# One planned order for loads, weights and the f32 loads of pairs 8 to 11, one release per pair, and x of batch 1 transposed on TensorE

## Chip, cores and metric

One core of one Trainium2 chip. The metric is the device time of an execution in microseconds. "Time" is the median of an execution's runs; "span" is the length of the profiled execution from its first to its last instruction, which in these runs is 1.8 us less than that same execution's time (321.0 and 322.81 for the kernel before). The profiled run of the kernel before is one of its slower ones, so spans and medians differ a little. Each ratio compares a kernel with the kernel before on the same chip in the same rounds. The experiments ran on four chips (runs 1 to 8, 9 to 15, 16 and 17, 18), and the changed kernel was timed only in the first comparison, so an experiment is set beside it by ratios, across rounds. Every experiment was correct unless it is said to be wrong on purpose.

## The reference

Attention with random positive features (32 pairs of heads), whose output is the input x of a two-layer network with a sigmoid gate:

```python
def phi(x):                                   # q and k scaled by D**-0.25
    proj = np.einsum('bhsd,md->bhsm', x, omega)   # 128 features of 64 columns
    h = proj - np.sum(x * x, axis=-1, keepdims=True) / 2.0
    return np.exp(h - np.max(h, axis=-1, keepdims=True)) / np.sqrt(m)
kv  = np.einsum('bhsm,bhsd->bhmd', k_p, v);  z = np.sum(k_p, axis=2)
num = np.einsum('bhsm,bhmd->bhsd', q_p, kv)
den = np.einsum('bhsm,bhm->bhs', q_p, z)[..., None] + 1e-06
# x = num / den, heads side by side: 4608 tokens x 512
h = x @ w_in                                  # 512 x 2048
return (h / (1.0 + np.exp(-1.702 * h))) @ w_out   # 2048 x 512
```

q, k and v are (8, 8, 576, 64), all f32.

## The kernel before

The kernel is made by a small planner in Python that runs when the kernel is built. It knows every operation, what it depends on, on which engines it can go and how long it takes there, and simulates the whole kernel. What it hands on is only the order of operations on each engine; on the chip each engine runs its own list strictly in order, and waits where data are missing.

One operation of the planner, by its name, for a pair i of heads: `hk`, `hq`, `hv` (f32 loads of k, q, v, pairs 8 on, issued by SyncE), `cast` (to bf16, ScalarE or VectorE), `TD` (q and k transposed by a DMA, issued by SyncE), `K`, `Q`, `KV`, `ND` (TensorE), `xm` (x of the pair into `xb`), `XD` (x transposed by a DMA into `xt`), `m1` and `m2` (four matmuls of the first and the second layer), `st` (a store, SyncE). `ld` are the loads that GpSimd issues: pairs 1 to 7 and the eight weight quarters `wi` and `wo`.

```python
QUEUE = {"hk": 4.5, "hq": 4.5, "hv": 4.5, "TD": 4.5, "XD": 3.0}  # issue to landing
ENGINES = {                                    # us on each engine that may do it
    "m1": {"P": 0.864}, "m2": {"P": 0.864},  # ... cut
    "TD": {"S": 1.6}, "XD": {"S": 1.2}, "st": {"S": 0.9},
    "hk": {"S": 0.9}, "hq": {"S": 0.9}, "hv": {"S": 0.9},
    "cast": {"D": 0.740, "A": 1.010},        # ... cut
}
LOADS = [("k", 1), ("q", 1), ("k", 2), ("q", 2), ("k", 3), ("q", 3), ("v", 0), ("v", 1), ("v", 2), ("v", 3)]
LOADS += [("wi", j) for j in range(4)]
LOADS += [(x, i) for i in range(4, 8) for x in "kqv"] + [("wo", j) for j in range(4)]
XDMA, TDMA = 6, 8          # from this pair on x, and q and k, are transposed by DMA
JOIN, AHEAD = 16, 2        # from this pair on Q, KV and K(+2) are one burst
# ... in schedule():
    deps["gate", 8] = [("ld", "wo", 0)]       # all f32 loads wait for w_out's first quarter
    for i in range(EARLY, NPAIR):
        deps["hk", i] = [("hv", i - 1) if i > EARLY else ("gate", 8)] + ([("cast", i - NSTG)] if i - NSTG >= EARLY else [])
        deps["cast", i] = [("hk", i), ("hq", i)] + [("TD" if i - NSTQ >= TDMA else "TQ", i - NSTQ)]
# ... issued from emit(), shortened:
def TD(i):                                     # runs on SyncE's queue
    nc.sync.dma_start_transpose(t[:], qk_t[i][:])
def XD(i):
    nc.sync.dma_start_transpose(dst, xb)
```

The softmax here doesn't subtract the row's maximum and nothing guards it: scores larger than these inputs give would overflow.

## Time and profile before

| | before |
|---|---|
| time, median of the runs | 320.94 us (319.98 to 322.03) |
| span of the profiled run | 321.0 us |
| TensorE busy, mean granted clock | 97%, 0.998 |
| DMA | 51.69 MB, 161 GB/s over the span |

The prediction below shows the page's slices, windows and waits and how to read them. One view it does not show is that of the DMA issues (what, queue, count, KB, median us from issue to landing):

```profile
win<-in_moe_w_in_dram POOLq DMA_DIRECT2D x4, 512.0 KB, 11.3
wout<-in_moe_w_out_dram POOLq DMA_DIRECT2D x4, 512.0 KB, 10.0
```

### The profile page before, as it was taken

Reading aid. Unit: us, or ns where it says so; the run is one execution under the profiler, and the core shown is the slowest. Engines: PE = TensorE matmul, PEld = TensorE weight load, DVE = VectorE, ACT = ScalarE, POOL = GpSimd, SP = SyncE. Lnnn points to the kernel's source line nnn. Section 1 sums busy time; section 2 is a strip of 40 time slices with the busy share of each in tenths; the row PEclk is TensorE's granted clock in tenths of the full one; section 3 lists DMA queues with packets and bytes.
Section 4 is the critical chain, followed back from the end, with each engine's and each line's share of the span. In section 5 each row is a group of like instructions: output and inputs, shape, how many; then the busy total and the mean of one; then the engine's idle time right before and its main releaser. Section 6 shows DMA issues by size and latency. Waiting matters only on the chain.

```text
span 321.0 us, 6636 instructions
## 1 busy us (share of the span) xinstructions
PE 310.8 (97%) x2567; PEld 152.2 (47%) x2567; DVE 179.6 (56%) x341; ACT 202.2 (63%) x379; POOL 59.9 (19%) x98
## 2 busy tenths in 40 slices
PE   6899999999999999999999999999999999999995
PEld 3565554444454444444444454444444444444444
DVE  2878854688558946574666556554635344344300
ACT  3957975788789667866688567666654434434411
POOL 8946311311131211111102030212010000000000
PEclk9999999999999999999999999999999999999999
DMA  8999989999999999999999472323022121111133
GB/s 171 271 222 263 207 253 306 146 300 259 285 191 239 261 242 251 243 237 266 289 263 257 71 134 39 74 54 88 20 56 53 35 59 39 35 33 34 33 88 78
DMA packets 69663, 51.69 MB, mean 161 GB/s; under 512 B 49024, under 2 KB 55168, under 8 KB 69632
## 3 DMA queue, kind: packets, MB, share of 16 engines
q1 hardware_dynamic: 62384, 42.25, 56.4%
q0 software_dynamic: 6880, 8.62, 13.8%
q8 instruction: 20, 0.33, 0.5%
q10 hardware_dynamic: 368, 0.39, 0.4%
q14 instruction: 11, 0.09, 0.1%
HBM read 36.73 MB, written 9.44 MB: 144 GB/s over the span
## 4 chain that ended last, share of the span: by engine, by line
PE 74%; DMA 16%; DVE 3%; issue 2%; ACT 2%; POOL 1%; SPq 1%; ACTq 0%; DVEq 0%; POOLq 0%
PE mo L695 17%; PE mo L721 16%; PE trB L721 12%; PE tr L695 8%; PE trB L695 6%; DMA stg<-in_q_dram 5%; PE tr L721 5%; DMA v<-in_v_dram 4%; DMA wout<-in_moe_w_out_dram 2%; PE nd L657 2%; PE nd L639 2%; DMA stg<-wout 2%; PE pqk L561 2%; DMA xt<-xb 1%; DMA om_f<-in_omega_dram 1%
## 5 line engine op out<-in xcount | busy, mean ns | idle before, releaser
L721 PEld LDWEIGHTS <-gT 128*128 128x128 bf16 x592 | 55.8, 98 | 61.9 <-issue 0.5
L695 PEld LDWEIGHTS <-win 128*128 128x128 bf16 x576 | 53.2, 98 | 61.3 <-issue 2.7
L695 PE MATMUL mo<-xt,win 128*128 128x512 bf16 x316 | 80.2, 379 | 0.4 <-DMA xt<-xb 0.3
L721 PE MATMUL mo<-wout,gT 128*128 128x512 bf16 (+1 forms) x304 | 71.4, 368 | 0.0
L705 ACT ACTIVATE th<-mo 128x512 bf16<-128x512 f32 x79 | 47.5, 606 | 33.9 <-PE mo L695 33.7
L709 DVE SCALAR_TENSOR_TENSOR gT<-th,mo 128x512 bf16<-128x512 bf16 x79 | 53.1, 677 | 27.6 <-ACT th L705 27.3
L721 PE MATMUL trB<-wout,gT 128*128 128x512 bf16 x208 | 51.6, 379 | 0.0
L627 POOL CAST vp<-em 128x9 bf16<-128x9 f32 x31 | 7.3, 235 | 167.8 <-DVE em L619 139.2
L628 POOL TENSOR_TENSOR vp<-v,em 128x576 bf16<-128x576 f32 x31 | 36.0, 1161 | 0.2 <-issue 0.2
L695 PE MATMUL tr<-xt,win 128*128 128x512 bf16 x132 | 33.9, 379 | 0.0
L709 DVE SCALAR_TENSOR_TENSOR gT<-th,tr 128x512 bf16<-128x512 bf16 x33 | 22.5, 681 | 20.3 <-ACT th L705 20.3
L579 ACT ACTIVATE ke<-pqk 128x1024 bf16<-128x1024 f32 x31 | 32.7, 1055 | 0.9 <-PE pqk L561 0.9
L695 PE MATMUL trB<-xt,win 128*128 128x512 bf16 x128 | 32.9, 379 | 0.3 <-DVE gT L709 0.3
L610 DVE TENSOR_TENSOR hm<-ke 128x576 bf16<-128x576 bf16 x32 | 15.8, 492 | 30.5 <-ACT ke L579 29.1
L705 ACT ACTIVATE th<-tr 128x512 bf16<-128x512 f32 x33 | 19.8, 599 | 20.3 <-PE tr L695 20.3
L709 DVE SCALAR_TENSOR_TENSOR gT<-th,trB 128x512 bf16<-128x512 bf16 x32 | 21.8, 680 | 9.9 <-ACT th L705 9.8
L705 ACT ACTIVATE th<-trB 128x512 bf16<-128x512 f32 x32 | 19.4, 608 | 11.4 <-PE trB L695 11.4
L674 DVE TENSOR_TENSOR xb<-nd,r 128x640 bf16<-128x640 f32 x30 | 24.3, 811 | 0.8 <-ACT qe L571 0.5
L614 DVE TENSOR_REDUCE m<-hm 128x9 f32<-128x576 bf16 x32 | 23.9, 747 | 0.3
L541 ACT ACTIVATE qk<-stg 128x1152 bf16<-128x1152 f32 x13 | 15.2, 1168 | 8.3 <-DMA stg<-in_q_dram 8.3
L721 PE MATMUL tr<-wout,gT 128*128 128x512 bf16 x80 | 19.6, 379 | 0.0
L543 DVE CAST qk<-stg 128x1152 bf16<-128x1152 f32 x11 | 8.3, 754 | 18.1 <-DMA stg<-in_q_dram 18.1
(83 smaller groups left out, 283.1 us busy)
## 6 DMA issues: line engine op xcount, KB each, us to landing
out_dram<-osb SPq DMA_DIRECT2D x70, 128.0 KB, 2.4
stg<-in_k_dram SPq DMA_DIRECT2D x25, 288.0 KB, 4.0
stg<-in_q_dram SPq DMA_DIRECT2D x24, 288.0 KB, 4.5
v<-in_v_dram SPq DMA_DIRECT2D x24, 288.0 KB, 4.0
v<-in_v_dram POOLq DMA_DIRECT2D x8, 288.0 KB, 5.6
win<-in_moe_w_in_dram POOLq DMA_DIRECT2D x4, 512.0 KB, 11.3
wout<-in_moe_w_out_dram POOLq DMA_DIRECT2D x4, 512.0 KB, 10.0
qk<-in_k_dram POOLq DMA_DIRECT2D x7, 144.0 KB, 5.6
```

What stands on the lines that cost most here:

```text
L541: nc.scalar.activation(out=dst, in_=src, func=AF.Copy)
L543: nc.vector.tensor_copy(out=dst, in_=src)
L579: nc.scalar.activation(out=st[i]["ke"][:, 1:9, :].rearrange("p (j e) f -> p e j f", e=2), in_=pk[:].rearrange("p e (j f) -> p e j f", f=12 ...
L610: nc.vector.tensor_tensor(out=hm[:], in0=ke[:, :, 0:64], in1=ke[:, :, 64:128], op=ALU.max)
L614: nc.vector.reduce_max(out=m[:], in_=st[i]["hm"][:], axis=AX.X)
L627: e.tensor_copy(out=t[:, :, 64], in_=em[:])
L628: e.tensor_tensor(out=t[:, :, 0:64], in0=v_t[i][:], in1=em[:].unsqueeze(2).to_broadcast([128, NS, 64]), op=ALU.mult,)
L674: nc.vector.tensor_tensor(out=xb[:].rearrange("p g e d -> p e g d"), in0=v4[:, :, :, 0:64], in1=r[:].unsqueeze(3).to_broadcast([128, 2, NG ...
L695: nc.tensor.matmul(dst, lhsT=win[:, c, f * 128 : (f + 1) * 128], rhs=xt[c][:, n * 512 : (n + 1) * 512], start=(c == 0), stop=(c == NC_ - 1),)
L705: nc.scalar.activation(out=t[:], in_=src, func=AF.Tanh, scale=0.851)
L709: nc.vector.scalar_tensor_tensor(out=gts[n][:, f, :], in0=t[:], scalar=1.0, in1=src, op0=ALU.add, op1=ALU.mult)
L721: nc.tensor.matmul(dst, lhsT=gts[n][:, f, m * 128 : (m + 1) * 128], rhs=wout[:, f, w], start=(f == 0), stop=(f == NFC - 1),)
```

## The change

The intent: start the f32 loads of pairs 8 to 11 earlier, between the weights, each pair released by its own load of the planned order; give SyncE's work the durations of a bare issue and model the DMA queue by its service rate (`RING`), so that SyncE's list can be packed tighter; do more attention before the first layer; join Q, KV and K into one burst from pair 8 on; transpose x of pairs 6 and 7 on TensorE. The core of the diff (start-up details, single turns and placements cut):

```diff
-QUEUE = {"hk": 4.5, "hq": 4.5, "hv": 4.5, "TD": 4.5, "XD": 3.0}
+RING = {"hk": 0.85, "hq": 0.85, "hv": 0.85, "TD": 1.1, "XD": 0.65, "st": 0.75}
-    "TD": {"S": 1.6},  "XD": {"S": 1.2},  "st": {"S": 0.9},
-    "hk": {"S": 0.9},  "hq": {"S": 0.9},  "hv": {"S": 0.9},
+    "TD": {"S": 1.4},  "XD": {"S": 1.3},  "st": {"S": 1.2},
+    "hk": {"S": 0.47}, "hq": {"S": 0.47}, "hv": {"S": 0.47},
-LOADS = [("k", 1), ("q", 1), ...                       # as above
+LOADS = "k1 q1 k2 q2 k3 v0 v1 v2 q3 k4 v3 v4 k5 q4 k6 v5 q5 wi0 k7 q6 v6 q7 v7 wi1 wo0 wi2 wi3 wo1 wo2 wo3"
-BEGIN, SPACING = 8, 8
-XDMA, TDMA = 6, 8
+BEGIN = [1, 4, 12, 12, 13, 14, 17, 25, 48, 59, 60, 73, ...]   # one per pair from 8 on
+GATES = {8: 17, 9: 17, 10: 26, 11: 29}                 # pair: number of the load that releases it
+XDMA, TDMA = 8, 8
-JOIN, AHEAD = 16, 2
+JOIN, AHEAD = 8, 2
@@ schedule()
-    deps["gate", 8] = [("ld", "wo", 0)]
+    for i, n in GATES.items():
+        deps["gate", i] = [("ld", *LOADS[n])]
...
+        if kind in RING:
+            busy = st["dma"] > start                   # are GpSimd's loads still coming?
+            if busy and kind not in ("TD", "XD"):
+                st["dma"] += RING[kind]                # loads delay them; transposes do not
+            st["hw"] = max(st["hw"], start + 1.3) + RING[kind] * ((6.0 if kind in ("TD", "XD") else 1.7) if busy else 1.0)
@@ gate()
-            nc.sync.dma_start(stg[EARLY][:].bitcast(BF16)[:, 2 * S : 2 * S + 2], wout[:, 0, 0:2])
+            nc.gpsimd.tensor_copy(out=stg[i][0:1, S : S + 2], in_=src)   # src: two numbers of the weight quarter
```

The planner's own end goes from 313.1 to 311.8 us. Neither is a measurement: the kernel before runs 8 us longer than its plan.

## The prediction

> **What bounds the kernel now.** I read the page's slices first (busy tenths of 40 slices of 8 us, by engine), then busy time by windows, then single matmuls in the timeline and the chain.
>
> ```profile
> PE   6899999999999999999999999999999999999995
> DVE  2878854688558946574666556554635344344300
> ACT  3957975788789667866688567666654434434411
> DMA  8999989999999999999999472323022121111133
> ```
> TensorE is busy from slice 3 to the end. DMA is full until about 180 us, but TensorE does not stand still for it, so full DMA is no proof of a bound. The windows (length; then each engine's busy us and instructions):
>
> ```profile
> 0.00:10.00 10.00, 7.43 (x48) 3.82 (x49) 3.07 (x12) 4.62 (x7) 8.65 (x19) 1.00 0.91 198
> 10.00:20.00 10.00, 8.30 (x166) 5.70 (x167) 9.79 (x24) 8.21 (x18) 8.17 (x13) 1.00 1.19 238
> 20.00:30.00 10.00, 9.88 (x78) 5.04 (x76) 7.01 (x13) 6.07 (x13) 5.67 (x10) 1.00 1.18 252
> 240.00:280.00 40.00, 40.00 (x195) 18.30 (x194) 17.35 (x26) 17.32 (x29) 0.00 (x0) 1.00 0.20 44
> ```
> From 10 to 20 us VectorE, the third pair, is at 9.79 of 10: it feeds TensorE there. Busy TensorE also counts drains and the dummy matmuls on zeros (L760), so I count work by spacing. In the chain four matmuls of 128x512 take 0.86 us, 0.216 each; the first four after attention work take 0.97:
>
> ```profile
> 160.18 0.86 PE tr L721 x4
> 161.04 0.32 PE trB L590
> 161.36 0.00 PE mo L590
> 161.36 0.29 PE nd L639 x18
> 161.65 0.22 PE pqk L561 x8
> 161.87 0.05 PE nd L566
> 161.93 0.00 PE nd L567
> 161.93 0.97 PE tr L721 x4
> ```
> Taking 0.216 for 512 columns and in proportion for fewer, a pair's attention costs 0.28 (K) + 0.216 (Q) + 0.28 (KV) + 0.31 (ND) = 1.09 us. Above, Q, KV and K in one burst took 161.93 - 161.04 = 0.89 plus 0.11 in the next group, 1.00 for 0.776 of work. Total work: 576 first-layer and 592 second-layer matmuls (32 of them half size) 248.8; 32 pairs x 1.09 = 34.8; transposes of q and k of eight pairs 4.0; transposes of x of six pairs 1.7: **289.4 us**. The last matmul ends at 317.35, so 28.0 us are not work, and 3.65 follow it (last eviction and store). Of those 28.0, start to next start less nominal in the timeline gives 6.9 in the first 10 us, 5.5 in the next 10, 4.5 from 20 to 60, 8.0 from 60 to 180, 1.9 after, and 1.2 before the first matmul. The largest single waits after 26 us are small:
>
> ```profile
> 52.14 0.46 PE L639 MATMUL nd<-vp,ke 64*128 64x65 bf16 x18 [0.49 <-POOL vp L628]
> 70.73 0.46 PE L639 MATMUL nd<-vp,ke 64*128 64x65 bf16 x18 [0.69 <-DVE xb L674]
> 127.77 1.02 PE L695 MATMUL trB<-xt,win 128*128 128x512 bf16 x4 [0.25 <-DVE gT L709]
> 156.35 1.24 PE L695 MATMUL mo<-xt,win 128*128 128x512 bf16 x5 [0.29 <-DMA xt<-xb]
> ```
> So the kernel is TensorE work plus a start (13.6 us) that VectorE and ScalarE set, plus some 10 us of seams, plus about 3.5 of waits.
>
> **What the Trainium skill says.** "TensorE: Matmul & The Clock Gate", section "Wait — 56ns, not 53.3ns?", gives 215.7 ns start to start for 512 columns, warm; the trace has 0.86/4. "TensorEngine Tiling (Array Packing)", section "Key Properties", says that changing the tiling mode drains the array. K and KV use 64-row tiles, and the trace agrees: median extra 0.096 us on entry (second layer to Q or K), 0.12 after K. "DMA: Bandwidth & Descriptors", section "Queues, rings and completion order", says that DMA engines go round robin between queue rows: hardware loads started early will slow the weights. No run shows that here yet; before, they wait until a small copy of the weights has landed:
>
> ```profile
> SPq L483 <- DMA stg<-wout: 5.9, 1, 5.9
> DMA to landing us min/median/max: 7.6/11.3/13.4
> ```
> (the second line is of the w_in loads.) From landings in the trace: a k, q or v tile every 0.735 us (pairs 4 to 7: 24.2 to 32.3 in 11 steps), a weight quarter every 2.55 us (w_out: 34.8 to 42.4 in 3).
>
> **The change part by part.**
>
> *Seams.* The instruction order of the changed kernel has 76 changes between 64-row and other work, against 96: Q, KV and K of pairs 8 to 15, till now in two places, become one burst (the joining starts at pair 8 instead of 16). I compare from the point where the third group of four first-layer matmuls starts, because from there on TensorE is nearly full in both. Before it is reached at 23.5 us, with 280.1 of work and 82 changes to come; with the measured transition medians the seams are 10.3 (0.126 each), together 290.4. 23.5 + 290.4 = 313.9 against 317.35: waits 3.5. After: 276.7 of work and 58 changes, 7.0, together 283.7. So 6.7 us less lies behind that point: 3.3 fewer seam microseconds and 3.3 us of attention work done earlier (K of pairs 4 to 6 and Q of 4 and 5 go ahead of it, pairs 3 to 7 before most of the first layer). The two more transposes of x (pairs 6, 7: 2 x 0.28 = 0.56) are in this sum.
>
> *The start.* Not free: more attention before the first layer means more VectorE and ScalarE work. k is loaded first and only its four blocks gate the first transposes, so I put the first transpose-copy at 5.2 us instead of 6.44 and the first exp at 6.7 instead of 7.9. The first maximum (L610) follows the two large exps and two small ones, 0.91 + 0.91 + 0.3 later, and copies queued: about 9.1, against 9.42. From there VectorE must run, up to the copy of x of pair 3 that the third group needs: six maxima x 0.37, six reductions x 0.66, two v products with their casts x 1.21, four products into xb x 0.74, evictions 640 wide 0.41 and 512 wide 0.33 (one and three), three copies of x x 0.37, two kvs x 0.19, reciprocals 0.13 to 0.25: 16.2 us, using issue intervals of the trace between 9 and 20 us. That is 25.3, then transposes' latency and the first matmuls: **26.3** for the point, if VectorE hardly idles (before it did not from 9.4 to 20.5). ScalarE gives the same: 18 us of exp and copies from 6.7 to its second tanh, 24.9 and some idle. So 2.8 of the 6.7 us are given back.
>
> *Loads.* In the new order w_in quarter 0 is 18th of the GpSimd loads; k1 lands at 5.75 before, so 16 steps x 0.735 + 2.55 = 20.1. The other quarters: w_in 1 at 26.3, w_in 2 at 31.4, w_in 3 at 33.9, w_out 3 at 41.6, plus what pairs 8, 9 (six tiles, 4.4 us) and 10 (2.2) take in between: 35.8, 38.3 and 48.2. TensorE, started at 26.3, gets to these needs at 26.3 + 8.0 = 34.3 (w_in 2), 38.0 (w_in 3), 48.1 (w_out 3). They meet within 1.5 us: the loads are about level with the work, not clearly ahead. The hardware loads start about 20 us earlier than at 41.2; later pairs do not wait for data in either kernel, so by itself this saves nothing after 80 us.
>
> *Sum.* 26.3 + 283.7 + waits 3.5 + tail 3.65 = **317.2 us**, taking the timed median as equal to the profiled span as before (320.94 and 321.0).
>
> **The rivals.** (1) *The start eats the gain.* The trade is attention before the first layer; if VectorE idles 2 us waiting for TensorE and ScalarE in turn, or its casts for pair 8 and the GpSimd products hold each other up, the point comes at 28.5 and the end at 319 to 320. For it: VectorE at 9.79 of 10 already. Against it: ScalarE takes three k evictions from it. (2) *Weights late.* Round robin gives pairs 8 to 10 more than their share; w_in 2 and 3 come 2 to 4 us late with nothing else to do, waits of 6 to 7 and 320 to 321. For it: arrivals above level with needs. Against: attention of pairs 6 to 9 can fill in. (3) *The plan fits better than the old one.* The old start lost 13.6 us with many dummies; with k first, the releases by pair and hand-made turns, DMA stops being late, the point comes at 25 and waits fall to 1.5: 25 + 283.7 + 1.5 + 3.65 = 313.9. For it: turns and beginnings of single pairs are plainly chosen to remove waits; against: VectorE's 16 us in series. (4) *Late waits*: x of pair 15 is finished only 6 us before block 3 begins (9.7 before), and the transposing DMA xt took 4.6 at worst: 1 us at most.
>
> **Range and chances.** Point 25.0 to 27.5 and waits 1.5 to 5.5 around 3.5, mostly independent: 313.8 to 320.7. Over 2% faster is under 314.5: rival 3 nearly whole, 0.20. Over 2% slower (327.4) would need a stall that nothing shows: 0.02. Else 0.78.
>
> **What would show it.** Right: the third first-layer group (its line moves from L695 to L744) starts at 25 to 27.5 us, more attention before it; VectorE over 9 of 10 from 10 to 24 us; 0.216 spacing unchanged; TensorE's other losses after that point 10 to 11 us instead of 13.8; first hardware load of pair 8 at 20 to 23 us. Wrong: the point at 23.5 or before (VectorE not the start's bound); waits on w_in or w_out of over 2 us between 30 and 50 (rival 2); or new waits after 60 us of over 3 us together.

## The result and the profile after

| | before | after |
|---|---|---|
| time, median (range) | 320.9 (319.98 to 322.03) | 331.23 (330.44 to 333.04) |
| span of the profiled run | 321.0 | 330.1 |
| third group of the first layer starts | 23.5 | 28.6 |
| last matmul ends | 317.3 | 326.2 |

The ratio is 1.0328, with a 95% interval of 1.0271 to 1.0385: slower. Ratios here are the mean time of one kernel's fast runs over that of the other's of the same rounds, so they are not quite the ratios of the medians.

**First the slices** (40 slices of 8.25 us, busy tenths; PEclk is the granted TensorE clock):

```profile
PE   8778898999998699999999999999999999999995
PEclk9999999999999599999999999999999999999999
DMA  8999998999998999988983454222131530111223
```

The prediction shows the PE and DMA rows of before. Counted from 0, TensorE now loses more in slices 1 to 4, in slice 6 and, new and largest, in slices 12 and 13 (99 to 116 us), and in slice 13 the clock also falls to about half.

**Where the time went.** To place losses I computed for both kernels, at many times, the end that would follow if TensorE never waited again: time, plus the nominal work still to come, plus the median cost of the changes of tiling still to come (my own working from the trace's spacings). Where this "projected end" rises, time is lost there. It is good to some 0.7 us: a recount with other medians moves single entries by that much.

| projected end at (us) | 28 | 45 | 60 | 80 | 105 | 120 | 310 |
|---|---|---|---|---|---|---|---|
| before | 315.4 | 314.7 | 315.1 | 315.8 | 315.8 | 316.0 | 317.1 |
| after | 312.8 | 315.6 | 316.2 | 317.4 | 318.8 | 325.2 | 326.0 |

At 28 us the changed kernel is 2.6 us **ahead**. It loses 2.8 us until 45, 3.2 more until 105, and 6.4 in fifteen us from 105 to 120.

**28 to 54 us: weights.** Median landing times after:

```profile
win<-in_moe_w_in_dram POOLq DMA_DIRECT2D x4, 512.0 KB, 14.3
wout<-in_moe_w_out_dram POOLq DMA_DIRECT2D x4, 512.0 KB, 23.8
```

The third and fourth quarter of w_in land at 39.4 and 42.7 us (predicted 35.8 and 38.3), the last of w_out at 54.2 (predicted 48.2; before 42.4). The windows of before and then of after say why (length, then busy us and instructions of PE, PEld, DVE, ACT, POOL, then the clock, the DMA share and GB/s; the share is the summed time of the packets over that of 16 engines, and can exceed 1):

```profile
35.00:40.00 5.00, 5.00 (x62) 2.59 (x62) 4.73 (x10) 4.33 (x8) 1.30 (x2) 1.00 1.27 207
40.00:45.00 5.00, 5.00 (x63) 2.67 (x57) 4.57 (x11) 3.31 (x8) 0.79 (x2) 1.00 0.83 207
45.00:50.00 5.00, 5.00 (x62) 2.66 (x61) 1.55 (x4) 4.57 (x8) 0.51 (x1) 1.00 1.00 345
```

```profile
35.00:40.00 5.00, 3.37 (x35) 1.72 (x35) 3.67 (x8) 4.78 (x9) 1.10 (x2) 1.00 1.27 183
40.00:45.00 5.00, 4.95 (x32) 2.27 (x30) 4.59 (x10) 3.17 (x6) 1.41 (x3) 1.00 1.25 186
45.00:50.00 5.00, 4.95 (x64) 3.02 (x65) 3.81 (x7) 4.08 (x9) 0.00 (x0) 1.00 1.29 169
```

The DMA engines are at least as full as before but move less. In the trace's packets from 35 to 40 us, 683 weight packets of 1024 bytes stand beside 668 transpose packets of 256 bytes: about one for one. The transposing DMAs of q and k of pairs 8 and 9 run there. Alone such a transpose takes 1.54 us (1152 packets, at 202 us); these two together take from 35.0 to 51.8 us, and a weight quarter behind them some 3.7 us instead of 2.5. Pairs 10 and 11 are released by weights, so they are late as well. The waits of GpSimd, after (us in total, times, longest):

```profile
POOL stg L533 <- DMA win<-in_moe_w_in_dram: 6.7, 1, 6.7
POOL stg L533 <- DMA wout<-in_moe_w_out_dram: 1.9, 1, 1.9
```

and the timeline of SyncE's queue, after:

```profile
30.93 10.33 SPq L558 DMA_TRANSPOSE qkT<-qk  x2
42.99 0.33 SPq L521 DMA_DIRECT2D stg<-in_k_dram  x1
...
54.41 0.33 SPq L521 DMA_DIRECT2D stg<-in_k_dram  x1
```

Between these SyncE stands: from 41 to 54 us it issues for 1.4 us, while the kernel before issues for 11.3 of the same 13.

**54 to 110 us: SyncE's order.** Here SyncE is busy nearly all the time in both kernels. What it gets done differs:

| SyncE, 54 to 110 us | k, q, v loads | TD | XD | stores | busy us |
|---|---|---|---|---|---|
| before: count | 9, 9, 9 | 9 | 9 | 12 | 51.4 |
| after: count | 12, 12, 11 | 10 | **4** | 14 | 50.2 |
| after: mean us of one | 0.51, 0.67, 0.49 | 1.77 | 1.29 | 0.56 | |
| in the changed plan | 0.47 each | 1.4 | 1.3 | 1.2 for two | |

A pair's loads and two transposes take 4.7 us by the measured means, 4.1 by the changed plan, and 5.5 by the old plan, which was on the safe side. So SyncE falls behind its list. Actual start minus planned start of SyncE's operations: before +4.6, +5.4 and +5.5 at 65, 95 and 105 us; after +7.9, +12.2 and +14.1. As the plan thought SyncE fast, it put prefetches far ahead: the XD of pair 11 stands behind the k loads up to pair 20 and the TDs up to 17 (before: 17 and 15).

**105 to 120 us: the stall.** Timelines of TensorE, ScalarE and SyncE, after:

```profile
105.73 0.81 PE L770 MATMUL mo<-wout,gT 128*128 128x512 bf16 x3 [0.16 <-issue]
110.51 1.87 PE L744 MATMUL tr<-xt,win 128*128 128x512 bf16 x4 [3.97 <-DVE gT L758]
```

```profile
102.19 0.60 ACT L754 ACTIVATE th<-mo 128x512 bf16<-128x512 f32 x1 [0.58 <-PE mo L744]
108.09 1.16 ACT L581 ACTIVATE qk<-stg 128x1152 bf16<-128x1152 f32 x1 [5.30 <-DMA stg<-in_q_dram]
109.16 0.58 ACT L754 ACTIVATE th<-tr 128x512 bf16<-128x512 f32 x1
```

```profile
102.84 0.43 SPq L521 DMA_DIRECT2D stg<-in_k_dram  x1
103.33 1.86 SPq L523 DMA_DIRECT2D stg<-in_q_dram  x1
```

Read from the bottom: q of pair 21 is issued at 103.33, 12.6 us after its planned time, and lands at 107.99. ScalarE's cast of pair 21 waits for it, 5.30 us, though by the plan K of pair 21 starts only 39 us after the cast. Behind the cast, in fixed order, stands a tanh that TensorE needs. TensorE stands 3.97 us, and then runs at half clock for 5 us and more (column before DMA share):

```profile
105.00:110.00 5.00, 1.39 (x33) 0.80 (x27) 0.22 (x1) 1.91 (x3) 1.30 (x2) 0.88 0.94 191
110.00:115.00 5.00, 4.49 (x20) 1.99 (x20) 2.95 (x6) 4.64 (x10) 0.00 (x0) 0.50 1.06 353
```

The Trainium skill, "TensorE: Matmul & The Clock Gate", section "What's actually happening", says that after an idle window of about 3.4 us the array gets half its clock until about 3.4 us of activity have passed. The trace agrees in the length of the half clock, not in the idle time that it takes. By the clock's records it lasts from 108.81 to 115.64 us, 6.83 us, so it begins 2.3 us into the stand; in runs 1, 2 and 5 it lasts 3.41 us at the stall, and in run 5 it follows a wait of only 2.34 us. Of the 6.4 us lost here 4.0 are the stand and about 2.4 the clock.

One wait, before and then after, shows that the harm is in single long waits, not in their number:

```profile
ACT qk L541 <- DMA stg<-in_q_dram: 8.3, 8, 2.2
```

```profile
ACT qk L581 <- DMA stg<-in_q_dram: 13.6, 7, 5.3
```

### The profile page after: what moved, and what is told of

The parts are those of the page before. It is cut to its first block, busy times and chain, and to the rows that moved or that the text cites. A ratio compares the mean times of both kernels' runs of the same rounds, so it can differ in the third digit from the quotient of the medians.

```text
span 330.1 us, 6649 instructions
## 1 busy us (share of the span) xinstructions
PE 308.7 (94%) x2548; PEld 154.8 (47%) x2589; DVE 180.5 (55%) x345; ACT 202.2 (61%) x386; POOL 58.6 (18%) x100
## 4 chain that ended last, share of the span: by engine, by line
PE 62%; DMA 19%; ACT 5%; DVE 4%; issue 3%; SPq 3%; POOL 2%; ACTq 0%; DVEq 0%; POOLq 0%
PE mo L770 15%; PE mo L744 13%; DMA stg<-in_q_dram 9%; DMA wout<-in_moe_w_out_dram 9%; PE tr L770 7%; PE trB L744 7%; PE tr L744 7%; PE trB L770 6%; PE nd L706 2%; PE nd L688 2%; DMA qk<-in_q_dram 2%; PE pqk L603 1%; ACT ke L626 1%; PE mo L639 1%; DVE gT L758 1%
## 5 line engine op out<-in xcount | busy, mean ns | idle before, releaser
L744 PE MATMUL mo<-xt,win 128*128 128x512 bf16 x282 | 72.7, 381 | 1.3 <-DVE gT L758 0.8
L758 DVE SCALAR_TENSOR_TENSOR gT<-th,mo 128x512 bf16<-128x512 bf16 x73 | 49.5, 680 | 30.9 <-ACT th L754 30.6
L754 ACT ACTIVATE th<-mo 128x512 bf16<-128x512 f32 x73 | 43.7, 602 | 35.2 <-PE mo L744 33.3
L744 PE MATMUL tr<-xt,win 128*128 128x512 bf16 x131 | 35.5, 387 | 4.6 <-DVE gT L758 4.0
L744 PE MATMUL trB<-xt,win 128*128 128x512 bf16 x141 | 38.3, 386 | 1.5 <-DMA win<-in_moe_w_in_dram 0.9
L770 PE MATMUL tr<-wout,gT 128*128 128x512 bf16 (+1 forms) x155 | 37.3, 368 | 0.3 <-issue 0.2
L758 DVE SCALAR_TENSOR_TENSOR gT<-th,trB 128x512 bf16<-128x512 bf16 x37 | 25.3, 683 | 20.7 <-ACT th L754 20.5
L677 POOL TENSOR_TENSOR vp<-v,em 128x576 bf16<-128x576 f32 x30 | 34.6, 1152 | 0.0
L754 ACT ACTIVATE th<-trB 128x512 bf16<-128x512 f32 x37 | 22.6, 612 | 16.7 <-PE trB L744 16.5
L770 PE MATMUL trB<-wout,gT 128*128 128x512 bf16 x126 | 31.8, 379 | 0.3 <-issue 0.2
L784 ACT ACTIVATE osb<-mo 128x512 f32<-128x512 f32 (+1 forms) x19 | 11.4, 599 | 13.8 <-PE mo L770 13.8
```

What stands on the lines that cost most here:

```text
L677: e.tensor_tensor(out=t[:, :, 0:64], in0=v_t[i][:], in1=em[:].unsqueeze(2).to_broadcast([128, NS, 64]), op=ALU.mult,)
L744: nc.tensor.matmul(dst, lhsT=win[:, c, f * 128 : (f + 1) * 128], rhs=xt[c][:, n * 512 : (n + 1) * 512], start=(c == 0), stop=(c == NC_ - 1),)
L754: nc.scalar.activation(out=t[:], in_=src, func=AF.Tanh, scale=0.851)
L758: nc.vector.scalar_tensor_tensor(out=gts[n][:, f, :], in0=t[:], scalar=1.0, in1=src, op0=ALU.add, op1=ALU.mult)
L770: nc.tensor.matmul(dst, lhsT=gts[n][:, f, m * 128 : (m + 1) * 128], rhs=wout[:, f, w], start=(f == 0), stop=(f == NFC - 1),)
L784: nc.scalar.activation(out=o[:, w], in_=src[:, 0 : w.stop - w.start], func=AF.Copy, scale=0.5)
```

## The experiments

Two theories. **A, order**: the changed durations let the planner stack prefetches ahead of needed transfers on SyncE, and fixed orders turn this into stalls. **B, capacity**: f32 loads and transposes among the weights leave a debt of DMA work, which any order meets before 130 us. Both started from narrower suspects, which the first runs were to tell apart. Eighteen kernels ran. The edits below are the core lines, shortened; the loops around them are cut.

### 1. One cast later

```diff
+    if o[0] == "cast" and o[1] == 21:           # planned time + 4.5: nine instructions later on ScalarE
+        s = max(s, min(s + 4.5, at["TD", o[1]] - 0.01, at.get(("hk", o[1] + NSTG), 1e9) - 0.01))
```

> The cast of pair 21 (f32 to bf16 on ScalarE) stands nine instructions later in ScalarE's order; nothing else moves. Theory A (a late load stops ScalarE in its fixed order, TensorE starves for 4.1 us at 106 us and is then clocked at half speed for some 7 us): the gap at 106 us goes, the clock digits stay at 9, and the time falls by 5 to 7 us, to 324.5 to 326. Rival D (the delay is elsewhere and the next fixed wait takes its place): the gap moves to another place and the time falls by less than 2 us.

331.86 us, 1.0325 (1.029 to 1.0361). Timelines of ScalarE and TensorE:

```profile
114.46 1.16 ACT L586 ACTIVATE qk<-stg 128x1152 bf16<-128x1152 f32 x1 [4.55 <-DMA stg<-in_q_dram]
```

```profile
116.88 1.44 PE L749 MATMUL trB<-xt,win 128*128 128x512 bf16 x3 [5.45 <-DVE gT L763]
```

The stall is not gone: it moved to the next cast, that of pair 22. The wait behind pair 21's cast was only where the lag first showed.

### 2. No transposing DMAs of pairs 8 and 9 (wrong on purpose)

```diff
+            if i < 10:                          # TD: copied untransposed on GpSimd
+                nc.gpsimd.tensor_copy(out=t[:].rearrange("p n c -> p (n c)"), in_=qk_t[i][:])
+                return
```

> Wrong result on purpose: the transposing DMAs of pairs 8 and 9 are replaced by GpSimd copies of the same tile, so that no 256-byte packets run beside the weight loads; every other instruction and its order stay. Theory A (transposes and weights alternate packet by packet and hold each other up): w_out's last quarter lands 4 to 6 us earlier than 54.2, so do the releases of pairs 10 and 11, K of pair 9 no longer waits for its transposed tile, and the time falls by 4 to 8 us (the stall at 106 shrinks too). Rival B (the start, bound by VectorE and ScalarE, and not the DMA, is what costs): landings change, the time by less than 2 us.

328.39 us, 1.0223 (1.0186 to 1.0259); relative error 0.043, as meant. The last weights land at 50.0 us instead of 54.2, and the projected end at 60 us is 314.7 (after: 316.2). So the two transposes cost the weights 4.2 us, and the kernel 1.5 us there; in all it is 3.4 us by the ratios, less than the 4 to 8 expected. The late stall stays:

```profile
106.96 1.65 PE L747 MATMUL tr<-xt,win 128*128 128x512 bf16 x4 [3.95 <-DVE gT L761]
```

### 3. Pairs 8 to 11 released by the last weight quarter

```diff
-GATES = {8: 17, 9: 17, 10: 26, 11: 29}
+GATES = {8: 29, 9: 29, 10: 29, 11: 29}
```

> The f32 loads of pairs 8 and 9 are released by the last weight quarter, as those of pair 11, instead of by the first; the kernel's own planner then orders all again. Theory A: the weights land as in the sum of the prediction, the last quarter at 41 to 43 us instead of 54; first and second layer work of blocks 0 and 1 no longer waits. As attention of pairs 8 and 9 comes later, the total falls by 3 to 6 us, if the new plan adds no wait. Rival B: same total within 2 us.

335.03 us, 1.0432 (1.0397 to 1.0467). The weights are all there at 43.2 us, as expected, and the projected end at 50 us is 313.1, the best of the first runs. The time missed both forecasts: it rose. But everything else is planned anew by this change (the plan's own end is 320), and it then loses 14 us between 50 and 120. It shows that the early loads were the cause of the late weights, and that waiting for the weights is not the cure.

### 4. Joining from pair 16 again

```diff
-JOIN, AHEAD = 8, 2
+JOIN, AHEAD = 16, 2
```

> The changed kernel with bursts of Q, KV and K joined from pair 16 on, as before, instead of from pair 8. Prediction: some 1.5 to 2.5 us more of seams, so 333. Rival C (a joined burst waits for the latest of three chains, so joining early costs waits between 60 and 110 us): the time falls by 3 us or more and the waits in 60 to 110 us with it. Theory A: within 2 us of the changed kernel either way.

333.86 us, 1.0384 (1.0342 to 1.0426): by the ratios 1.8 us slower than the changed kernel, with overlapping intervals. The joining earns something, as the prediction had it, and is no cause of the loss.

### 5. All casts of pairs 10 and later up to 5 us later

```diff
+    if o[0] == "cast" and o[1] >= 10:
+        s = max(s, min(s + 5.0, at["TD", o[1]] - 0.01, at.get(("hk", o[1] + NSTG), 1e9) - 0.01))
```

> All casts of pairs 10 to 31 stand up to 5 us (of the plan's time) later in the order of VectorE and ScalarE, never after their transposing DMA or after the load that takes their buffer; nothing else moves. If the 4 us gap of TensorE near 106 us (111 us with one cast moved) is the fixed order of ScalarE holding on to a late load, not the data being needed, it goes and no other comes: 331.5 falls to 325 to 327. If the SP queue itself is too late for TensorE's own needs (theory Q), the wait moves to K and to the transposed tiles, and the time stays within 2 us of 331.5.

328.6 us, 1.0248 (1.0193 to 1.0304). Now it is the transpose of x that is missing (TensorE's timeline):

```profile
99.39 0.38 PE L749 MATMUL tr<-xt,win 128*128 128x512 bf16 x1 [2.34 <-DMA xt<-xb]
```

This is the XD of pair 11, issued at 96.65 us behind the TDs of pairs 16 and 17. With the casts out of the way, SyncE's order itself is seen.

### 6 to 8. v loads from GpSimd's queue

```diff
-                return load_v(i)                # pairs 8 and later, SyncE
+                return load_v(i, nc.gpsimd)
```

In the changed kernel, in the changed kernel with the later casts of run 5, and in the kernel before:

> The f32 loads of v of pairs 8 to 31 are issued by GpSimd instead of SP; all else and all orders stay. SP was issuing in 24.2 of 26 us from 54 to 80 and in 21.5 of 25 from 80 to 105; v took 0.5 us of it a pair. Theory Q (the SP queue, idle from 31 to 43 and 44 to 54 us because the releases come late, is then full to 125 us and is what delays the loads): k and q loads are issued 4 to 6 us earlier by 100 us, the gap at 106 shrinks to under 1 us, time 324 to 327. Theory DMA (the 16 DMA engines are full, whoever issues): loads land no earlier, time within 2 us of 331.5.

> Both edits. If they take away the same loss (the stall near 106 and the half clock after it), about as the better of the two; if they add, 321 to 324. The front (weights at 54 us) is untouched, so not under 319.

> The kernel before, with v of pairs 8 to 31 issued by GpSimd. Its own waits after 46 us are only 3 us together, so under theory Q it can win 1 to 2 us at most: 319 to 322; under theory DMA nothing, 321.

335.51 us (330.74 to 338.01), 330.24 (325.3 to 334.51) and 321.88 (320.99 to 325.51); ratios 1.0358, 1.0176 and 1.0036 (0.9971 to 1.0102). Two of the four runs of each of the first two were slow, and so were both their profiled runs; the fast runs took 330.74 and 335.08, and 325.3 and 328.78 us. Taking 24 issues off SyncE did not help. In the first, v of pairs 8 and 9 queues behind the weights (it lands at 43.7 and 49.3 us, in the changed kernel at 31.4 and 36.7); in the second's profile, of a slow run, there is a wait of 4.5 us for `xt`. Inconclusive on A.

### 9. Runs 2 and 5 together (wrong on purpose)

> Wrong result on purpose (pairs 8 and 9), the edits of e2_no_td and e5_all_casts together. Alone they took 3.1 and 2.9 us from 331.5. If the early transposes beside the weights and the casts' place in ScalarE's order are two separate losses, 325 to 326; if they are one loss seen twice (both are only the SP queue's lag), 328.

327.29 us (324.34 to 328.74), 1.0168. Little is lost until 110 us (projected end 314.2 to 315.4, with one wait of 1.1 us for x at 96 us), then there are waits of 0.9, 1.1 and 2.2 us, the last for x again. The early loss goes with the two transposes; the late one does not.

### 10. Both last quarters of w_in ahead of w_out

```diff
+                a = {("wo", 0): ("wi", 2), ("wi", 2): ("wi", 3), ("wi", 3): ("wo", 0)}.get(a, a)
```

> The four loads w_out 0, w_in 2, w_in 3 take each other's places: w_in 2 and 3 first, then w_out 0; nothing else moves. TensorE stood for w_in 2 at 39.4 us. Then w_in 2 lands at 35 and w_in 3 at 39.5, the ninth first-layer group starts at 36.5 to 37.5 instead of 39.4, and pair 10 is released 3 us earlier. But w_out 3, landing at 54, still holds the second layer, so if the front's loss is set by the last quarter, the total gains under 1 us; if by w_in 2, 2 to 3 us.

330.5 us, 1.0287 (1.0263 to 1.0311): 1.3 us less than the changed kernel by the ratios, with overlapping intervals, and the stall, now 4.1 us from 105.0, is there with its half clock.

### 11. Loads and TDs of pairs 12 and later 4 us later on SyncE

> In SP's order the f32 loads and transposes of q and k of pairs 12 to 31 stand 4 us (of the plan) later, so that transposes of x and stores come relatively earlier; casts up to 8 us later. Theory: after 54 us SP carries prefetches for pairs that are needed 15 to 40 us later ahead of transposes of x that TensorE needs now; this alone turns SP's lag into waits. Then neither the 106 us stall nor the 2.5 us wait for x of pair 11 (seen with casts later) comes: 323.5 to 326. If SP or the DMA engines are simply too slow for the whole, waits move to K: 328 to 331.

332.08 us, 1.0324 (1.028 to 1.0367). The wait moved to K at 92.0 us (3.0 us), as the TDs of pairs 12 to 15 had no 4 us to give. Badly chosen: it does not tell A from B.

### 12. Prefetches of pairs 16 and later just in time

```diff
+    for i in range(16, NPAIR):                  # times by which each list is sorted
+        at["TD", i] = max(at["TD", i], at["K", i] - 12.0)
+    for i in range(16, NPAIR):
+        at["cast", i] = max(at["cast", i], at["TD", i] - 4.5, at["TD", i - NSTQ] + 0.01)
+        t = max(at["hk", i], at["TD", i] - 10.5, at["cast", i - NSTG] + 0.01)
+        for n, x in enumerate(("hk", "hq", "hv")):
+            at[x, i] = max(at[x, i], t + 0.01 * n, at["hv", i - 1] + 0.01 if n == 0 else 0)
```

> The changed kernel with one thing moved: for pairs 16 and later the loads of k, q, v, the cast and the transposing DMA of k and q stand as late in their engines' orders as the planned use allows (transposing DMA 12 us before K, cast 4.5 us before that, loads 10.5 us before that). All other work keeps its planned place. In SyncE's order the transposing DMA of pair 11's x then stands behind the k loads up to pair 16 and the transposing DMAs up to 15 (20 and 17 in the changed kernel; 17 and 15 in the kernel before). Theory (prefetches that stand ahead of needed transfers in SyncE's fixed order cause the stall near 105 us and the half clock after it): no TensorE wait of over 1.5 us between 90 and 130 us, the projected end stays at 318 to 320 from 80 us to the end, time 321 to 325, ratio to the kernel before 1.00 to 1.01. Rival (the DMA engines are short of capacity until 130 us whatever the order): the stall moves again, as it did when only casts were moved; 328 to 332.

326.42 us, 1.0163 (1.0135 to 1.019). TensorE's largest wait between 90 and 130 us is 1 us, and the clock never falls (page, slices; TensorE's timeline):

```profile
PEclk9999999999999999999999999999999999999999
```

```profile
104.83 1.02 PE L754 MATMUL tr<-xt,win 128*128 128x512 bf16 x4 [0.98 <-DVE gT L768]
```

SyncE's lag at 105 us is +8.0 instead of +14.1, with the same loads, the same weights and the same start. The projected end is 317.2 at 105 us and 317.9 at 120. The engines of all operations are the same as well. That is A, for the stall; the time came 1.4 us above the range, half the loss was left.

### 13. The kernel before, with the changed durations

```diff
-    "TD": {"S": 1.6}, "XD": {"S": 1.2}, "st": {"S": 0.9}, "hk": {"S": 0.9}, "hq": {"S": 0.9}, "hv": {"S": 0.9},
+    "TD": {"S": 1.4}, "XD": {"S": 1.3}, "st": {"S": 1.2}, "hk": {"S": 0.47}, "hq": {"S": 0.47}, "hv": {"S": 0.47},
```

> The kernel before, with only the six durations of SyncE's work in the planner set to the changed kernel's (loads 0.47 instead of 0.9 us, transposing DMAs 1.4 for 1.6 and 1.3 for 1.2, stores 1.2 for 0.9). The instructions are the same, their order changes: the transposing DMA of pair 11's x now stands behind the k loads up to pair 21 and the transposing DMA of q and k of pair 17, as in the changed kernel (before: 17 and 15). Start, seams up to pair 15, gates and weights stay as before. Theory (SyncE's order, from durations that are too short, is what costs the 6 us after 100 us): stalls of 3 us or more together between 90 and 130 us, time 325 to 330, ratio 1.012 to 1.028. Rival (the loss needs the early loads of pairs 8 to 11 beside the weights): within 0.7% of the kernel before, no stall over 1.5 us.

**335.29 us, 1.0406** (1.0349 to 1.0463). This is the test that B cannot pass: no f32 load between the weights, no release by pair, the old start, the same operations, and yet it is at least as slow as the whole change (one of its four runs was slow; the fast ones took 332.52 to 336.12 us). Not the order alone differs, though: the planner also chose the other one of VectorE and ScalarE for fifteen casts, in both directions, and one copy. Its plan ends at 313.0, the same as before. SyncE's timeline, VectorE's and TensorE's:

```profile
99.08 0.42 SPq L483 DMA_DIRECT2D stg<-in_k_dram  x1
99.56 0.42 SPq L485 DMA_DIRECT2D stg<-in_q_dram  x1
100.08 1.20 SPq L524 DMA_TRANSPOSE xt<-xb  x1
```

```profile
101.49 0.76 DVE L543 CAST qk<-stg 128x1152 bf16<-128x1152 f32 x1 [5.15 <-DMA stg<-in_q_dram]
```

```profile
104.26 0.59 PE L695 MATMUL tr<-xt,win 128*128 128x512 bf16 x1 [2.98 <-DMA xt<-xb]
```

k and q of pair 21 are issued ahead of the transpose of pair 11's x, and TensorE waits 2.98 us for that x; the VectorE line is the cast of pair 20, which waits for its q in the same way. In the kernel before, the same transpose goes out at 89.64, behind k of pair 17. SyncE's lag grows to +17.2 at 105 us. Losses begin with a wait of 3.0 us for ScalarE that ends at 51.4 and sum to 13.5 from 45 to 105 us, so more than I expected (325 to 330).

### 14 and 15. Later prefetches, without the two transposes, and with the weights' order

> Wrong on purpose (like the earlier kernel without the transposing DMAs of pairs 8 and 9, whose q and k then are copied untransposed on GpSimd), and with the later order of pairs 16 and on. If the two causes are separate and add up, the loss at 35 to 45 us and the loss at 105 to 120 us both go: projected end 314 to 316 from 50 us on, time 317 to 320, ratio 0.985 to 1.00. If the transposes beside the weights matter only through the late order, it is no faster than the later order alone (321 to 325). If order does not help, 327 or more, as with both earlier undoings.

> The later order of pairs 16 and on, together with the third and fourth quarter of the first weight matrix loaded ahead of the first quarter of the second. Alone the swap gave about 0.9 us. Theory: both parts add, 320 to 324, ratio 0.997 to 1.008, no correctness change. If the weights' order decides nothing once the late stall is gone, it equals the later order alone within 1 us.

322.86 us, 1.0052 (1.0019 to 1.0084; wrong on purpose), and 325.32 us, 1.0124 (1.0098 to 1.015). By the differences of the ratios (1% is 3.2 us) undoing both causes gives 8.9 of the 10.5 us back, where run 2 alone gave 3.4 and run 12 alone 5.3: they add. The weights' order gives about 1 us on top of run 12. Both last times came above what I expected; each profile still has a wait for x near 189 us (1.9 us in the first).

### 16 and 17. Plans with measured durations, searched anew

Planner with SyncE's durations 1.9 (TD), 1.25 (XD) and 0.9 (a load), service times of the queue 15% longer, and transposes counted against the weights; load order, releases, beginnings, turns and some engines (in the second also JOIN 12) found by random search, judged by the plan and by a replay (on the host, no measurement) of each engine's fixed list with slower service.

> A version that is meant to beat both. The changed kernel's planner with SyncE's durations set to what the traces show with the queue's waiting in them (loads 0.9, transposing DMAs of q and k 1.9, of x 1.25 us), the queue's service times 15% longer, and transposing DMAs counted against the weights; then load order, releases, beginnings and turns searched anew for that planner and for a replay of the fixed orders with queue service times 0, 12 and 22% longer. The replay puts the changed kernel at 323 to 331 us (330.1 measured), this one at 315.0 to 315.6. Theory (the wrong durations of DMA and SyncE made the plan go wrong): no wait of over 1.5 us on TensorE from 60 us on, 316 to 321 us, ratio to the kernel before 0.985 to 1.00. Rival (what is missing is DMA capacity, which a plan cannot give): a stall near 100 us again and 325 or more.

> The same planner and search from another start: in its SyncE order the transposing DMA of pair 11's x stands behind the k loads up to pair 15 and the transposing DMAs up to 14 (20 and 17 in the changed kernel, 17 and 15 before), and pairs 8 to 11 are released by the first quarter of w_in for pair 8 on: 8 late, 9 to 11 close together. Replay 314.1 to 314.7. Theory: 315 to 320, no stall over 1.5 us from 60 us on. Rival: as for the other one.

328.39 us, 1.0191 (1.0162 to 1.022) and 325.19 us, 1.0135 (1.0082 to 1.0188). Both miss the time. The replay had been good on the changed kernel and was 9 to 12 us short here. The largest waits of TensorE, in the first and then in the second, are before 46 us:

```profile
PE mo L745 <- DMA win<-in_moe_w_in_dram: 3.1, 1, 3.1
PE nd L707 <- ACT kvs L582: 2.9, 1, 2.9
```

```profile
PE mo L745 <- DVE gT L759: 2.1, 1, 2.1
PE mo L745 <- DMA win<-in_moe_w_in_dram: 1.2, 2, 1.0
```

From 60 us on they lose 1.3 and 1.0 us of projected end (after: 9.8; before: 2.0). So the late part of A held, and my new starts were worse than the changed kernel's.

### 18. The changed start, and measured durations from 50 us on

```diff
+LATE, RATE, STRETCH = 50.0, {"TD": 1.9, "XD": 1.25, "hk": 0.9, "hq": 0.9, "hv": 0.9}, 1.15
+        if start > LATE:
+            dur = RATE.get(kind, dur)          # queue service times x STRETCH likewise
# and beginnings, turns and the engine of the casts of pairs 12 and later searched anew; weights' order as in run 10
```

> The changed kernel up to 47 us, instruction for instruction (but the third and fourth quarter of the first weight matrix loaded ahead of the first quarter of the second), and from planned time 50 us on a plan made with SyncE's durations as the traces show them (transposing DMA of q and k 1.9, of x 1.25, loads 0.9 us) and queue service times 15% longer, with beginnings and turns of pairs 12 and later searched anew for it. Its own planned end is 311.8, the same as the changed kernel's. Theory (start costs what it costs in the changed kernel, the late loss goes as in the two corrected plans, which lost 1.0 and 1.3 us after 60 us): projected end 315 to 316 at 60 us and 316 to 317.5 at the end, no wait over 1.5 us after 60 us, time 319 to 322.5, ratio 0.993 to 1.003, so level with the kernel before. Rival (the start leaves a debt of DMA work that any late order meets again): a wait of 2 us or more between 90 and 130 us, 324 or more.

320.63 us (320.21 to 321.45; before in the same rounds 321.39), ratio 0.9984 (0.996 to 1.0009), as expected: level with the kernel before, and 10.6 us under the changed kernel (medians of different rounds), with which it shares the order of all operations planned before 47 us, but for three weight quarters. Its plan ends at 311.8, exactly like the changed kernel's. The page's slices and TensorE's largest waits:

```profile
PE   7778998999999999999999999999999999999995
PEclk9999999999999999999999999999999999999999
```

```profile
PE pqk L811 <- DVE zero L802: 1.2, 1, 1.2
PE pqk L606 <- DMA qkT<-qk: 1.1, 1, 1.1
PE tr L736 <- ACT qkT L584: 1.1, 1, 1.1
```

SyncE's lag stays between +0.5 and +4.1 us from 55 to 130 us. The projected ends of the deciding runs together:

| projected end at (us) | 28 | 45 | 105 | 120 | 310 |
|---|---|---|---|---|---|
| before | 315.4 | 314.7 | 315.8 | 316.0 | 317.1 |
| after | 312.8 | 315.6 | 318.8 | 325.2 | 326.0 |
| 12, prefetches just in time | 311.8 | 314.6 | 317.2 | 317.9 | 319.3 |
| 13, before with changed durations | 315.1 | 314.3 | 327.8 | 329.2 | 328.8 |
| 14, as 12 without two transposes | 312.1 | 314.4 | 315.4 | 316.2 | 318.0 |
| 18, late durations measured | 312.4 | 314.2 | 315.2 | 314.9 | 314.3 |

Run 18 shows that the change's own parts leave no debt that order cannot deal with: B falls for the part after 50 us. Its profiled run is 2.6 us shorter in span than that of before, yet the medians differ by 0.8 us only, as the profiled run of before was a slow one; I claim no gain for it.

## Why the prediction was wrong

Predicted 317.2 (313.8 to 320.7), measured 331.23: outside, and in the wrong direction. By its steps, in the profiled run: start 28.6 instead of 26.3 (+2.3), 283.7 as predicted, waits 13.9 (326.2 - 28.6 - 283.7) instead of 3.5 (+10.4), and 3.9 of tail: 330.1. **The term that failed is the 3.5 us of waits**, taken over from the kernel before (where they were nearer 2.2, see Seams).

- **The start** was put too early by 2.3 us. The first rival ("the point comes at 28.5 and the end at 319 to 320") had it; whether for its reason was not tested. By the projected end it was still a gain of 2.6 us over before.
- **Seams**: nothing contradicts the 283.7. One count for the kernel before was wrong: I left out the matmuls of Q, which run in 64-row tiles too (64*128 in the trace). Where Q stands alone they are two more changes; after the start of the third group the trace of before has 92, not 82 (after: 58 as counted; in all 110 and 78, not 96 and 76). At 0.126 each its seams are 11.6 us instead of 10.3 and its waits 2.2 instead of 3.5, so a correct sum would have forecast an even faster kernel, near 316. The projected ends here count them. Before the waits come, the projected end is 312.8, and run 4 without the joining is 1.8 us slower, though with overlapping intervals.
- **Loads.** "the loads are about level with the work" was right in form and 4 to 6 us off in size. I charged the weights with the pairs' loads but not with their transposes. These took 16.8 us in turns with the weights, and without them the last weight lands 4.2 us earlier (run 2). The second rival named round robin and put w_in 2 and 3 2 to 4 us late; they came 3.6 and 4.4 us after the forecast. 2.8 us were lost from 28 to 45.
- **The failed step** is the sentence "later pairs do not wait for data in either kernel, so by itself this saves nothing after 80 us", with rival 4's "1 us at most". It read the old trace's small waits as a property of the kernel. They were a property of its order, whose durations of 0.9 us per load and 1.6 per TD had held SyncE's list back to what the DMA could carry. The diff showed these six numbers cut, and I priced only instructions, none of which they add. Alone they make the kernel before 4% slower (run 13). After 45 us the changed kernel lost 10.4 us of projected end, and with measured durations from 50 us on 0.1 (run 18).
- **What I said would show me wrong** did: "new waits after 60 us of over 3 us together" (one of 4.0), and, less clearly, waits on the weights of over 2 us: 2.8 us of projected end were lost from 28 to 45, though the view of waits names only 0.9 us of `win`.

**Still open.** Run 18 changes durations, queue service times, beginnings, turns, one swap of weights and the engines of seven casts at once (six go from ScalarE to VectorE, that of pair 21 among them), so the 10.6 us are not split among these; run 13 splits the durations off in the kernel before only, and run 12 the order of prefetches in the changed one. The model of the queue by `RING` was never tried without the new durations. Whether a correct kernel without the two transposes beside the weights would beat both was not tried.

## What to carry to other kernels

In a kernel whose engines run fixed lists, a duration in the planner is a statement about order: check it against the mean in the trace **under load**, and compare planned with actual start times of the queue that issues DMAs. A lag that grows along the span is a warning long before a stall shows. A wait that moves to the next instruction when its first victim is moved (runs 1 and 5) says that the cause lies upstream, in the list that issues the data; and small transpose packets beside weight loads cost more than their bytes: the two transposes delayed the weights by 4.2 us (run 2), while their 0.59 MB at the weights' rate of 512 KB in 2.55 us would be 2.9 (an estimate).

## What the Trainium skill lacked or had wrong

- "DMA: Bandwidth & Descriptors", section "Latency and other measured facts", gives a DMA transpose 261 GB/s, or 350 to 400 in the contiguous case. Here one transpose of 128 x 1152 bf16 within on-chip memory, with nothing beside it, took 1.54 us for 294,912 bytes: 192 GB/s. But two others, whose issues ended over 1 us before their packets began (at 66.6 and 69.0 us), ran in 1.05 us each: 281 GB/s. So the runs do not show the page's figure to be wrong; it lacks this difference.
- The same page, section "Queues, rings and completion order", has the round robin of engines between queue rows at packet granularity. The trace fits it (683 packets of 1024 bytes beside 668 of 256 bytes in 5 us). It lacks the consequence: two transposes that need 3.08 us alone took 16.8 us beside weight loads, and delayed the last weights by 4.2 us.
- No page that I read has what a DMA costs the queue that issues it when the DMA engines are full: on SyncE from 54 to 110 us a transpose of q and k held the queue for 1.77 us (up to 2.57), against 1.3 after 180 us; a load 0.49 to 0.67, with single ones up to 1.86.
